# Attention state as four products of 144 columns over zeros, and the second route finished ahead of the third

## Chip, cores and metric

The kernel runs on one NeuronCore of a Trainium2 chip. The metric is device microseconds of one execution. Engines are named as in the profile: PE is TensorE (PEld its weight loads), DVE VectorE, ACT ScalarE, POOL GpSimd, SP SyncE.

## What is computed

Three layers follow one another: attention with a decay per head and no softmax (4 batches, 8 heads, 576 positions, 64 columns a head), a routed expert layer (2304 tokens of 512, 8 experts of width 1024, the best one only), and a gated FFN of width 1536.

```
scores = scale * np.matmul(q, k.transpose(0, 1, 3, 2))
Dmat = np.where(rel >= 0, gamma[:, None, None] ** rel[None, :, :], 0.0)
x = np.matmul(scores * Dmat, v)           # -> (2304, 512)
...
xn = x / (norm(x) + 1e-06)                # expert_idx = argmax(xn @ en.T / tau)
out[mask] = gate_w[mask, None] * (np.maximum(x[mask] @ w1[e], 0.0) @ w2[e])
...
return (silu(x @ w_gate) * (x @ w_val) @ w_out)
```

## The kernel before

**Attention.** A batch's 576 positions are cut into five chunks, four of 128 and one of 64 (c = 0 to 4), so that there are 20 chunks in all. The eight heads form four pairs (NP = 4): the pair's two heads of 64 columns lie on partitions 0 to 63 and 64 to 127 of q and k. The decay is put into two factors, `dk` on v's rows and `dq` on the output's rows. Beside the 64 columns of v each head carries 8 columns with its part of the expert logits (HE = 72), which `votes` makes.

For a chunk, `qk` (L231) makes the scores of all heads and VectorE multiplies them by the causal mask into `pd` (L244). `state` (L284) adds the chunk's k and v into a state in PSUM, and ScalarE copies it to SBUF as `sd` (L297), two buffers in turn. `rows` (L247) makes the output of the chunk: for c > 0 the queries times the state of the chunks before (L261), eight products, one for each head on its own 64 partitions, then the chunk's own scores times v (L265). VectorE then evicts the logits (L279), the rows (L281) and sums the logits over the heads (L282). PE instructions on float32 appear in the trace twice for each product written, each with a weight load.

**Order.** The schedule is written out by hand: `tc.manual_schedule()` keeps each engine's instructions in the order of the Python program. Step i of the main loop (L608) runs qk(i), votes, rows(i - 1), state(i), the preparation of v for chunk i + 2 on GpSimd (L215) and the load of chunk i + 5 on SyncE's queue, six chunk buffers in all.

**Routes.** A `Route` takes some chunks of a batch to their places in the experts' lists. `choose` (L316) finds the expert of each token on VectorE, after the root of the sum of squares on GpSimd (L325). `rank` counts the tokens ahead of each on PE. `place` turns that into row numbers, `weigh` makes the gate weight, and `scatter` (L392) sends the rows of a chunk out with one indirect DMA of GpSimd. The last batch is split into three routes: chunks 0 and 1, within the loop; 2 and 3 (`rb`); and 4 (`rc`). Where several generators are given to `run`, they are issued in turns, an instruction of each.

**After the attention.** `warm` issues bf16 products whose result is not used, 18 behind the last rank, 20 behind the branch that follows. SyncE then loads the first expert's rows, which waits for all scatters; the rows are scaled, transposed (L736) and split into two float32r parts. Eight experts and the FFN follow.

Of the kernel before, what the change touches and what calls it, by code (L numbers as in the profile page):

```python
# [4 lines left out]
F32 = mybir.dt.float32  # L5
# [47 lines left out]
def build(tc, main, tail, emb, wexp, keep, small, lim, wffn, out):  # L53
# [116 lines left out]
    sd = [ac.tile([P, NP, HE], F32, name=f"sd{i}") for i in range(2)]  # L170
# [60 lines left out]
    def qk(i):  # L231
        c = i % NC_
        L = CH[c][1]
        t = ck[i]
        t["pd"] = []
        scs = [ps_sc.tile([P, NP, P], F32, tag="sc", name="sc") for _ in range(2)]
        for p in range(NP):
            for a, sc in enumerate(scs):
                r = slice(64 * a, 64 * a + 64)
                nc.tensor.matmul(sc[keys(c, a), p, :L], t["k"][r, p], t["q"][r, p], start=True, stop=True)  # L240
        for a, sc in enumerate(scs):
            ks = keys(c, a)
            pd = ap.tile([P, NP, P], F32, tag=f"pd{a}", name="pd")
            nc.vector.tensor_tensor(out=pd[ks, :, :L], in0=sc[ks, :, :L], in1=causal[ks, P - L if a else 0:P if a else L].unsqueeze(1).to_broadcast([L, NP, L]), op=ALU.mult)  # L244
            t["pd"].append(pd)

    def rows(i, pool=None):  # L247

        b, c = divmod(i, NC_)
        L = CH[c][1]  # L250
        t = ck[i]
        if pool:
            parts = [pool.tile([P, 1, 512], F32, tag="sc", name="po") for a in range(2)]
# [12 lines left out]

        t = bt[b]
        lw = ap.tile([P, 2, NP, E], F32, tag="lw", name="lw")
        xv = t["xr"][:L, c, 0:D].rearrange("l (p a d) -> l a p d", p=NP, a=2)
        dqv = dq_s[:L, c].rearrange("l (p a) -> l a p", a=2)  # L270
        at = 0
        todo = []
        for x in parts:
            m = x.shape[1]
            s = slice(at, at + m)
            at += m
            view = x[:L, :, 0:NP * HE].rearrange("l a (p w) -> l a p w", p=NP)
            todo.append((xv[:, s], view[:, :, :, 0:HD], dqv[:, s].unsqueeze(3).to_broadcast([L, m, NP, HD])))
            nc.vector.tensor_tensor(out=lw[:L, s], in0=view[:, :, :, HD:HE], in1=dqv[:, s].unsqueeze(3).to_broadcast([L, m, NP, E]), op=ALU.mult)  # L279
        for o, x, y in todo:  # L280
            nc.vector.tensor_tensor(out=o, in0=x, in1=y, op=ALU.mult)  # L281
        nc.vector.tensor_reduce(out=t["lg"][:L, c], in_=lw[:L].rearrange("l a p e -> l e a p"), axis=AX.XY, op=ALU.add)  # L282

    def state(i):  # L284
# [12 lines left out]
        nc.scalar.activation(out=sd[(i + 1) % 2], in_=st, func=AF.Copy)  # L297
# [11 lines left out]
    class Route:  # L309


        def __init__(self, b, lo, hi):
            self.b, self.lo, self.n = b, lo, hi - lo
            self.L = max(CH[c][1] for c in range(lo, hi))

        def choose(self):  # L316
# [5 lines left out]
            mx, cm, dn, nrm = (ap.tile([P, NC_], F32, tag=x, name=x)[:L, :n] for x in ("mx", "cm", "dn", "nrm"))  # L322
# [15 lines left out]
            self.ex, self.dn, self.nrm = ex, dn, nrm  # L338
# [234 lines left out]
    with tc.manual_schedule():  # L573
# [10 lines left out]
        nc.gpsimd.memset(enb, 0.0)  # L584
        nc.scalar.activation(out=ej, in_=emb_s, func=AF.Square, accum_out=ess[:, 0:1])
# [22 lines left out]
        for i in range(N - 1):  # L608
# [59 lines left out]
        run(rc.weigh(), look_far(ac))  # L668
# [228 lines left out]
def _constants():  # L897
# [7 lines left out]
    dk = g[None, None, :] ** -at.astype(np.float64)  # L905
    dq = sc * g[None, None, :] ** at
# [55 lines left out]
```

## Times and profile before

| | us |
|---|---|
| runs of the kernel before | 819.76, 818.22, 823.55 (median 819.76) |
| the profiled execution's own time | 825.41 |
| its span, first to last instruction | 823.7 |
| granted clock of PE, mean of the span | 0.985 |

The profile is of one execution. Times in its rows count from the start of the span. [...] Busy times on PE overlap, as products are pipelined, so the spacing of starts says more than the sum.

### The profile page before, as it was taken

The numbers are of one execution on the slowest core, as the hardware profiler recorded it, in microseconds if no ns is written. First come the engines' busy times: TensorE is split into PE (matmuls) and PEld (weight loads), VectorE is DVE, ScalarE is ACT, GpSimd is POOL, SyncE is SP. The second block draws the span as 40 slices with busy tenths as digits, with TensorE's granted clock in tenths as the row PEclk, the third lists the DMA queues.
The fourth block names the chain that finished last, engine by engine and source line by source line (L and its number), as shares of the span: only waits on it lengthen the run. The fifth ranks groups of instructions, "written<-read, shape, count | busy, mean of one in ns | idle before, by whom it ended". The sixth has DMA issues, their size and how long they took to land.

```text
span 823.7 us, 14428 instructions
## 1 busy us (share of the span) xinstructions
PE 793.0 (96%) x5861; PEld 742.3 (90%) x5862; DVE 452.9 (55%) x866; ACT 258.8 (31%) x486; POOL 155.0 (19%) x154
## 2 busy tenths in 40 slices
PE   8897978999999999999999999999999999999995
PEld 5887838999999999999999999999999999999994
DVE  3565657566556566677744742772476356323322
ACT  2121226445444444444433311331232122111110
POOL 3354423111121011122201200120021011001122
PEclk9999989999999999999999999999999999999998
DMA  9999246554564454332211200120021000000121
GB/s 351 383 317 318 105 144 218 182 186 132 167 208 139 163 192 145 128 103 103 78 52 42 87 26 1 62 92 1 2 101 52 1 26 1 1 1 38 39 77 76
DMA packets 30312, 93.47 MB, mean 113 GB/s; under 512 B 5053, under 2 KB 5182, under 8 KB 30242
## 3 DMA queue, kind: packets, MB, share of 16 engines
q1 hardware_dynamic: 25552, 81.83, 29.2%
q0 software_dynamic: 4240, 9.85, 3.3%
q8 instruction: 47, 0.77, 0.3%
q10 hardware_dynamic: 450, 0.84, 0.3%
q14 instruction: 23, 0.19, 0.1%
HBM read 82.00 MB, written 11.97 MB: 114 GB/s over the span
## 4 chain that ended last, share of the span: by engine, by line
PE 71%; issue 17%; DMA 4%; DVE 3%; POOL 3%; ACT 0%; POOLq 0%; ACTq 0%; SPq 0%; DVEq 0%
PE po L862 13%; PE pg L750 9%; PE pg L751 9%; PE pg L749 9%; PE py L749 5%; PE py L750 4%; PE py L751 4%; PE ph L749 4%; PE ph L751 4%; PE ph L750 4%; DMA xs<-xr,slot 2%; PE po L265 2%; PE sc L240 2%; POOL out L870 2%; PE po L261 1%
## 5 line engine op out<-in xcount | busy, mean ns | idle before, releaser
L750 PE MATMUL pg<-yl,w 128*128 128x384 f32 x576 | 193.0, 335 | 0.0
L751 PE MATMUL pg<-yh,w 128*128 128x384 f32 x576 | 192.7, 335 | 0.0
L749 PE MATMUL pg<-yh,w 128*128 128x384 f32 x576 | 192.7, 335 | 0.0
L862 PE MATMUL po<-w,hh 128*128 128x512 f32 x432 | 135.7, 395 | 0.0
L852 DVE TENSOR_TENSOR hf<-pg,hf 128x384 f32<-128x384 f32 x72 | 40.2, 558 | 172.6 <-PE pg L751 168.4
L750 PEld LDWEIGHTS pg<-yl,w 128*128 128x128 f32 x576 | 108.1, 188 | 3.0
L749 PEld LDWEIGHTS pg<-yh,w 128*128 128x128 f32 x576 | 108.1, 188 | 2.9
L136 POOL TENSOR_TENSOR w<-w,w 128x512 fp32r<-128x512 f32 x36 | 50.8, 1410 | 310.7 <-DVE hl L854 235.7
L751 PEld LDWEIGHTS pg<-yh,w 128*128 128x128 f32 x576 | 108.1, 188 | 0.0
L114 DVE TENSOR_TENSOR w<-raw,w 128x1024 fp32r<-128x1024 f32 x64 | 78.3, 1224 | 36.3 <-ACT w L113 35.0
L862 PEld LDWEIGHTS po<-w,hh 128*128 128x128 f32 x432 | 80.3, 188 | 13.5 <-ACT hh L853 0.3
L851 ACT ACTIVATE hf<-pg 128x384 f32<-128x384 f32 x72 | 35.5, 493 | 169.2 <-PE pg L751 169.2
L853 ACT ACTIVATE hh<-hf 128x384 fp32r<-128x384 f32 x72 | 38.0, 527 | 159.2 <-DVE hf L852 159.2
L862 PE MATMUL po<-w,hl 128*128 128x512 f32 x216 | 85.6, 396 | 0.0
L749 PE MATMUL py<-hh,w 128*128 128x320 f32 x256 | 81.6, 319 | 0.0
L750 PE MATMUL py<-hl,w 128*128 128x320 f32 x256 | 79.8, 312 | 0.4 <-DVE hl L767 0.4
L751 PE MATMUL py<-hh,w 128*128 128x320 f32 x256 | 79.8, 312 | 0.0
L749 PE MATMUL ph<-xh,w 128*128 128x320 f32 x252 | 77.9, 309 | 0.0
L750 PE MATMUL ph<-xl,w 128*128 128x320 f32 x252 | 77.8, 309 | 0.0
L751 PE MATMUL ph<-xh,w 128*128 128x320 f32 x252 | 77.8, 309 | 0.0
L113 ACT ACTIVATE w<-raw 128x1024 fp32r<-128x1024 f32 x64 | 66.8, 1055 | 25.2 <-PE py L751 16.7
L854 DVE TENSOR_TENSOR hl<-hf,hh 128x384 fp32r<-128x384 f32 x72 | 40.2, 559 | 42.8 <-ACT hh L853 42.8
(133 smaller groups left out, 1118.7 us busy)
## 6 DMA issues: line engine op xcount, KB each, us to landing
raw<-wexp SPq DMA_DIRECT2D x64, 512.0 KB
raw<-wffn SPq DMA_DIRECT2D x36, 512.0 KB
ck<-main SPq DMA_DIRECT2D x32, 512.0 KB
xrow<-xs SPq DMA_DIRECT2D x16, 257.0 KB
ck<-main SPq DMA_DIRECT2D x16, 256.0 KB
ck<-tail SPq DMA_DIRECT2D x4, 512.0 KB
xrow<-xs SPq DMA_DIRECT2D x8, 128.5 KB
ck<-tail SPq DMA_DIRECT2D x4, 256.0 KB
```

What stands on the lines that cost most here:

```text
L113: nc.scalar.activation(out=w[:, 0], in_=raw, func=AF.Copy)
L114: nc.vector.tensor_tensor(out=w[:, 1], in0=raw, in1=w.bitcast(F32)[:, 0], op=ALU.subtract)
L136: nc.gpsimd.tensor_tensor(out=w[:, 1, i], in0=ff, in1=w.bitcast(F32)[:, 0, i], op=ALU.subtract)
L240: nc.tensor.matmul(sc[keys(c, a), p, :L], t["k"][r, p], t["q"][r, p], start=True, stop=True)
L749: nc.tensor.matmul(ps, w[0], ah, start=start, stop=False)
L750: nc.tensor.matmul(ps, w[0], al, start=False, stop=False)
L751: nc.tensor.matmul(ps, w[1], ah, start=False, stop=stop)
L851: nc.scalar.activation(out=hf, in_=pss[0], func=AF.Silu)
L852: nc.vector.tensor_tensor(out=hf, in0=pss[1], in1=hf, op=ALU.mult)
L853: nc.scalar.activation(out=hh, in_=hf, func=AF.Copy)
L854: nc.vector.tensor_tensor(out=hl, in0=hf, in1=hh.bitcast(F32), op=ALU.subtract)
L862: nc.tensor.matmul(po[t], h[a][:, s], w[:, c, f], start=(f == 0 and i == 0), stop=(f == 1 and i == 2))
```

## The change

The state in SBUF gets a place for both heads of a pair side by side, with zeros where a head's columns meet the other head's partitions. So one product of the pair's 128 partitions with 144 moving columns gives both heads, four products where there were eight. ScalarE copies the state in two halves; GpSimd zeroes both buffers at the start. The output's heads lie four to a PSUM bank in their order, instead of even heads in one and odd in the other. In the last chunk of a batch both heads' masked scores share one tile of 128 partitions, `dk` has zeros for the other head, and here too four products of 144 columns take the place of eight of 72.

The second change is in the routes of the last batch. The root is a step of its own (`root`), issued for the second route ahead of the first route's last scatter, which moves from step 18 to the steps behind the loop. The second route's choice stands ahead of the last chunk's rows; its place, weight and scatters come ahead of the third route's choice.

```diff
-    sd = [ac.tile([P, NP, HE], F32, name=f"sd{i}") for i in range(2)]
+    sd = [ac.tile([P, NP, 2, HE], F32, name=f"sd{i}") for i in range(2)]
...
+            if a == 0 or c < NC_ - 1:
+                pd = ap.tile([P, NP, P], F32, tag=f"pd{a}", name="pd")
...
-        bank = [x[:, a, 0:NP * HE].rearrange("l (p w) -> l p w", p=NP) for x in parts for a in range(x.shape[1])]
+        bank = [x[:, n, 0:4 * HE].rearrange("l (h w) -> l h w", w=HE) for x in parts for n in range(x.shape[1])]
         if c:
             for p in range(NP):
-                for a in range(2):
-                    r = slice(64 * a, 64 * a + 64)
-                    nc.tensor.matmul(bank[a][:L, p], t["q"][r, p, :L], sd[i % 2][r, p], start=(p == 0), stop=False, skip_group_check=True)
-        for p in range(NP):
-            for a in range(2):
-                for m in HALVES[:L // 64]:
-                    nc.tensor.matmul(bank[a][m, p], t["pd"][a][keys(c, a), p, m], t["vd"][keys(c, a), 2 * p + a], start=(c == 0 and p == 0), stop=(p == NP - 1), skip_group_check=True)
+                nc.tensor.matmul(bank[p // 2][:L, 2 * (p % 2):2 * (p % 2) + 2], t["q"][:, p, :L], sd[i % 2][:, p], start=(p % 2 == 0), stop=False, skip_group_check=True)
+        for p in range(NP):
+            o = bank[p // 2][:, 2 * (p % 2):2 * (p % 2) + 2]
+            if c < NC_ - 1:
                 for a in range(2):
+                    for m in HALVES:
+                        nc.tensor.matmul(o[m, a], t["pd"][a][:, p, m], t["vd"][:, 2 * p + a], start=(c == 0 and p % 2 == 0 and a == 0), stop=(p % 2 == 1), skip_group_check=True)
+            else:
+
+                nc.tensor.matmul(o[:L], t["pd"][0][:, p, :L], t["vd"][:, 2 * p:2 * p + 2], start=False, stop=(p % 2 == 1), skip_group_check=True)
...
-        nc.scalar.activation(out=sd[(i + 1) % 2], in_=st, func=AF.Copy)
+        for a in range(2):
+            r = slice(64 * a, 64 * a + 64)
+            nc.scalar.activation(out=sd[(i + 1) % 2][r, :, a], in_=st[r], func=AF.Copy)
...
+        def root(self):
+
+            if self.nrm is None:
+                n, L = self.n, self.L
+                self.nrm = ap.tile([P, NC_], F32, tag="nrm", name="nrm")[:L, :n]
+                nc.gpsimd.tensor_tensor(out=self.nrm, in0=bt[self.b]["ss"][:L, self.lo:self.lo + n], in1=half[:L, :n], op=ALU.pow)
...
-            nc.gpsimd.tensor_tensor(out=nrm, in0=t["ss"][:L, cs], in1=half[:L, :n], op=ALU.pow)
+            self.root()
...
+        for x in sd:
+            nc.gpsimd.memset(x, 0.0)
...
-                    at_step(i + 1 + (n if b < B - 2 else n // 2), lambda r=r, n=n: r.scatter(n))
+                    at_step(i + 1 + (n // 2 if b == B - 2 else n), lambda r=r, n=n: r.scatter(n))
 
         rb, rc = Route(B - 1, 2, 4), Route(B - 1, 4, 5)
         rows(N - 2)
         squares(N - 2)
+        rb.root()
         for fn in later.pop(N - 1, ()):
             fn()
+
+        run(rb.choose())
         rows(N - 1, ps_sc)
-        run(rb.choose())
         squares(N - 1)
         rb.rank()
-        run(rc.choose(), rb.place())
-        rc.rank(ps_sc)
-        run(rb.weigh(), rc.place(1))
+        rc.root()
+        run(rb.place(), rb.weigh())
         rb.scatter(0)
         rb.scatter(1)
-        run(rc.weigh(), look_far(ac))
+        run(rc.choose())
+        rc.rank(ps_sc)
+        run(rc.place(2), rc.weigh(), look_far(ac))
         rc.scatter(0)
         warm(WARM[1], ps_1.tile([P, 512], F32, tag="st", name="warm"))
...
+    half = (i[:, None] < P // 2) == (np.arange(H)[None, :] % 2 == 0)
+    dk[:, NC_ - 1] *= half
```

## Rows read from the trace of the kernel before

**Rows 1.** The page: busy us of the engines (part 1), instruction queue (part 3).
```profile
PE 793.0 (96%) x5861; PEld 742.3 (90%) x5862; DVE 452.9 (55%) x866; ACT 258.8 (31%) x486; POOL 155.0 (19%) x154
...
q8 instruction: 47, 0.77, 0.3%
```

**Rows 2.** Busy by stretch: length, busy (instructions) per engine, PEclk, DMA share, GB/s.
```profile
20.32:26.44 6.12, 5.51 (x121) 5.08 (x122) 2.42 (x6) 1.12 (x3) 3.37 (x5) 1.00 1.03 401
72.45:79.74 7.29, 5.60 (x126) 5.14 (x126) 3.49 (x9) 1.75 (x5) 2.96 (x6) 1.00 0.95 330
79.74:86.77 7.03, 6.54 (x126) 6.00 (x126) 4.28 (x15) 1.02 (x3) 2.23 (x2) 0.76 0.69 249
86.77:93.20 6.43, 5.81 (x125) 5.18 (x125) 3.12 (x18) 1.27 (x4) 2.45 (x3) 1.00 0.12 45
```

**Rows 3.** PE's waits, 14 to 90 us: waiter, waited for, total us, times, longest.
```profile
PE po L265 <- issue: 2.3, 3, 0.9
PE pu L224 <- issue: 2.2, 2, 1.7
PE po L261 <- issue: 1.7, 1, 1.7
PE pr L364 <- issue: 1.6, 1, 1.6
PE st L296 <- DVE vd L225: 1.1, 1, 1.1
PE sc L240 <- issue: 0.8, 2, 0.4
```

**Rows 4.** PE in order of time (start, length, what): rows of chunks 16, 19.
```profile
89.42 1.02 PE L261 MATMUL po<-sd,ck 64*128 64x72 f32 x16
90.36 1.22 PE L265 MATMUL po<-vd,pd 128*64 128x72 f32 x32
...
101.53 0.72 PE L261 MATMUL po<-sd,ck 64*64 64x72 f32 x16
102.08 0.67 PE L265 MATMUL po<-vd,pd 64*64 64x72 f32 x16
```

**Rows 5.** PE's transposes of the first rows: in time; the tile's list (ns min/median/max).
```profile
118.29 0.60 PE L736 MATMUL ptx<-keep_s,xrow 128*128 128x128 f32 x4
...
L736 PE MATMUL ptx<-keep_s,xrow x12: 222/272/328, 118.3 to 120.4; 128*128 128x128 f32 x8, 64*128 64x64 f32 x4
```

**Rows 6.** In order of time: ACT's state copy, POOL at the start; brackets: idle before.
```profile
4.78 0.57 POOL L586 TENSOR_TENSOR ess<-ess,half 8x1 f32<-8x1 f32 x1 [2.95 <-ACT ej L585]
21.98 0.53 POOL L633 MEMSET zrow<- 128x514 f32 x1
61.61 0.41 ACT L297 ACTIVATE sd<-st 128x288 f32<-128x288 f32 x1 [2.67 <-PE st L296]
```

**Rows 7.** In order of time: the end of attention, the warm products, the last transposes.
```profile
102.38 0.26 DVE L282 TENSOR_REDUCE lg<-lw 128x8 f32<-128x64 f32 x1
104.05 0.15 DVE L326 TENSOR_REDUCE mx<-lg 128x2 f32<-128x16 f32 x1
105.09 0.18 PE L364 MATMUL pr<-oh,tri_s 128*128 128x8 bf16 x1 [2.34 <-DVE cm L332]
106.49 6.93 PE L571 MATMUL warm<-ones 128*128 128x512 bf16 x18
107.69 0.15 DVE L354 RECIPROCAL xr<-sm 128x2 f32<-128x2 f32 x1
110.75 0.92 POOL L394 DMA_INDIRECT xs<-xr,slot  x1 [0.30 <-issue]
113.94 4.51 PE L571 MATMUL warm<-ones 128*128 128x512 bf16 x20 [0.52 <-PEq L478]
120.14 0.46 PE L736 MATMUL ptx<-keep_s,xrow 64*128 64x64 f32 x4 [0.62 <-DVE xrow L705]
```

**Rows 8.** Busy by stretch, columns as in rows 2: most of the 18 warm products.
```profile
105.56:112.37 6.81, 6.09 (x16) 2.21 (x16) 4.50 (x30) 2.43 (x4) 3.34 (x4) 0.50 0.31 106
```

More of the change, by code (lines that the diff above doesn't have):

```diff
@@ L242, in qk @@
             ks = keys(c, a)
-            pd = ap.tile([P, NP, P], F32, tag=f"pd{a}", name="pd")
+            if a == 0 or c < NC_ - 1:
+                pd = ap.tile([P, NP, P], F32, tag=f"pd{a}", name="pd")
             nc.vector.tensor_tensor(out=pd[ks, :, :L], in0=sc[ks, :, :L], in1=causal[ks, P - L if a else 0:P if a else L].unsqueeze(1).to_broadcast([L, NP, L]), op=ALU.mult)
-            t["pd"].append(pd)
+            if a == 0 or c < NC_ - 1:
+                t["pd"].append(pd)
     def rows(i, pool=None):
@@ L252, in rows @@
         if pool:
-            parts = [pool.tile([P, 1, 512], F32, tag="sc", name="po") for a in range(2)]
+            parts = [pool.tile([P, 1, 512], F32, tag="sc", name="po") for _ in range(2)]
         else:
             parts = [ps_1.tile([P, 2, 512], F32, tag="po", name="po")]
-        bank = [x[:, a, 0:NP * HE].rearrange("l (p w) -> l p w", p=NP) for x in parts for a in range(x.shape[1])]
+        bank = [x[:, n, 0:4 * HE].rearrange("l (h w) -> l h w", w=HE) for x in parts for n in range(x.shape[1])]
         if c:
             for p in range(NP):
+                nc.tensor.matmul(bank[p // 2][:L, 2 * (p % 2):2 * (p % 2) + 2], t["q"][:, p, :L], sd[i % 2][:, p], start=(p % 2 == 0), stop=False, skip_group_check=True)
+        for p in range(NP):
+            o = bank[p // 2][:, 2 * (p % 2):2 * (p % 2) + 2]
+            if c < NC_ - 1:
                 for a in range(2):
-                    r = slice(64 * a, 64 * a + 64)
-                    nc.tensor.matmul(bank[a][:L, p], t["q"][r, p, :L], sd[i % 2][r, p], start=(p == 0), stop=False, skip_group_check=True)
-        for p in range(NP):
-            for a in range(2):
-                for m in HALVES[:L // 64]:
-                    nc.tensor.matmul(bank[a][m, p], t["pd"][a][keys(c, a), p, m], t["vd"][keys(c, a), 2 * p + a], start=(c == 0 and p == 0), stop=(p == NP - 1), skip_group_check=True)
+                    for m in HALVES:
+                        nc.tensor.matmul(o[m, a], t["pd"][a][:, p, m], t["vd"][:, 2 * p + a], start=(c == 0 and p % 2 == 0 and a == 0), stop=(p % 2 == 1), skip_group_check=True)
+            else:
+                nc.tensor.matmul(o[:L], t["pd"][0][:, p, :L], t["vd"][:, 2 * p:2 * p + 2], start=False, stop=(p % 2 == 1), skip_group_check=True)
         t = bt[b]
-        lw = ap.tile([P, 2, NP, E], F32, tag="lw", name="lw")
-        xv = t["xr"][:L, c, 0:D].rearrange("l (p a d) -> l a p d", p=NP, a=2)
-        dqv = dq_s[:L, c].rearrange("l (p a) -> l a p", a=2)
+        lw = ap.tile([P, 2, 4, E], F32, tag="lw", name="lw")
+        xv = t["xr"][:L, c, 0:D].rearrange("l (n h d) -> l n h d", n=2, h=4)
+        dqv = dq_s[:L, c].rearrange("l (n h) -> l n h", n=2)
         at = 0
@@ L276, in rows @@
             at += m
-            view = x[:L, :, 0:NP * HE].rearrange("l a (p w) -> l a p w", p=NP)
-            todo.append((xv[:, s], view[:, :, :, 0:HD], dqv[:, s].unsqueeze(3).to_broadcast([L, m, NP, HD])))
-            nc.vector.tensor_tensor(out=lw[:L, s], in0=view[:, :, :, HD:HE], in1=dqv[:, s].unsqueeze(3).to_broadcast([L, m, NP, E]), op=ALU.mult)
+            view = x[:L, :, 0:4 * HE].rearrange("l n (h w) -> l n h w", h=4)
+            todo.append((xv[:, s], view[:, :, :, 0:HD], dqv[:, s].unsqueeze(3).to_broadcast([L, m, 4, HD])))
+            nc.vector.tensor_tensor(out=lw[:L, s], in0=view[:, :, :, HD:HE], in1=dqv[:, s].unsqueeze(3).to_broadcast([L, m, 4, E]), op=ALU.mult)
         for o, x, y in todo:
             nc.vector.tensor_tensor(out=o, in0=x, in1=y, op=ALU.mult)
-        nc.vector.tensor_reduce(out=t["lg"][:L, c], in_=lw[:L].rearrange("l a p e -> l e a p"), axis=AX.XY, op=ALU.add)
+        nc.vector.tensor_reduce(out=t["lg"][:L, c], in_=lw[:L].rearrange("l n h e -> l e n h"), axis=AX.XY, op=ALU.add)
     def state(i):
@@ L321, in choose @@
             r8b = r8_s[:L].unsqueeze(1).to_broadcast([L, n, E])
-            mx, cm, dn, nrm = (ap.tile([P, NC_], F32, tag=x, name=x)[:L, :n] for x in ("mx", "cm", "dn", "nrm"))
+            mx, cm, dn = (ap.tile([P, NC_], F32, tag=x, name=x)[:L, :n] for x in ("mx", "cm", "dn"))
             cd, ex = (ap.tile([P, NC_, E], F32, tag=x, name=x)[:L, :n] for x in ("cd", "ex"))
             oh = self.oh = ap.tile([P, NC_, E], BF16, tag="oh", name="oh")[:L, :n]
-            nc.gpsimd.tensor_tensor(out=nrm, in0=t["ss"][:L, cs], in1=half[:L, :n], op=ALU.pow)
+            self.root()
             nc.vector.tensor_reduce(out=mx, in_=lg, axis=AX.X, op=ALU.max)
@@ L337, in choose @@
             yield
[L338 removed]
+            self.ex, self.dn = ex, dn
         def weigh(self):
```

1 line of the change is left out of this document (added).

## Prediction

> **What bounds the kernel now.** I read the page first, then a table of busy time by stretch, then TensorE's own waits, then the instructions in order of time at two places. The page gives TensorE (PE) 96% of the span [rows 1]. That average holds two different stages: from about 120 us on the expert and FFN products follow each other closely and nothing of the change touches them; up to about 103 us the attention chunks run, and there the change acts. So I look at the first stage alone.
>
> In the table by stretch the reader should look at the counts, not at the busy time: between one standstill of PE and the next lie about 126 products and 126 weight loads, each time, whatever the products are [rows 2]. The table of PE's waits says what ends these standstills: of 9.7 us between 14 and 90 us, 8.6 stand under "issue" (the engine waited for nothing that the profile shows), 1.1 under VectorE, none under a transfer of q, k or v [rows 3]. The page has one more line that fits: the queue q8 brought 47 packets of instructions, 0.77 MB, while PE ran 5861 products and 5862 loads in all; that is 249 instructions for each packet [rows 1], and 252 lie between two standstills (semaphore instructions make up the small rest). I take it that PE runs out of instructions: in this stage a block of some 250 takes as long as the next one needs to arrive. Three of these blocks measure 6.12, 7.29 and 7.03 us; from 20.32 to 86.77 there are ten, 66.45 us, 6.64 each [rows 2]. Without the 9.7 us of waits PE would execute a block in 5.7 us. In the block after 86.77 the DMA share is 0.12 instead of 0.69 or more, and PE is busy for 5.81 of 6.43 us where it was 5.60 of 7.29 [rows 2]: from there I take it as bound by what it executes.
>
> [...]
>
> **The change, part by part.**
>
> *Products of the state (c = 1 to 3, twelve times).* Before, eight products of 72 columns, recorded as 16; 0.94 us from the first to the next line's first [rows 4]. After, four products of 144 columns over 128 rows, recorded as 8. A float32 product over the whole array is seen at the transposes: four of 128 columns take 0.60 us from the first start to the last end, and one alone 0.272, so their starts lie 0.109 apart and those of 144 columns would lie 0.122 apart [rows 5]; eight make 0.98. They no longer have the tile shape of the score products ahead of them. A change of shape costs between nothing and one product, 0.12; I take 0.1. Sum: +0.14 each.
>
> [...]
>
> *The last chunk of a batch (c = 4, four times).* Before, the state's 16 take 0.55 and those with the scores, by the same spacing, 0.50 [rows 4]. After, both kinds are eight of 0.122: 1.96. Sum: +0.9 each.
>
> *Instructions.* Each record has its weight load, so c = 1 to 3 drop 16 instructions and c = 4 drops 32. Up to 86.77 us the rows of nine chunks with c = 1 to 3 and three with c = 4 have run: 9 x 16 + 3 x 32 = 240 fewer, 0.95 of a block.
>
> *Sum from 20.32 to 86.77.* If arrival alone set the pace, 0.95 x 6.64 = 6.3 us would go. Execution grows, though: 66.45 - 9.7 = 56.8 us, plus 8 x 0.14 and 3 x 0.9 (one of the nine ran earlier), is 60.6 for 9.05 blocks, 6.7 each. Arrival and execution come out nearly equal, and each block takes the longer of the two; as the blocks with c = 4 execute longer than the others, I add 0.1: 9.05 x 6.8 = 61.5, a gain of 4.9. Bounds: 60.1 (all of arrival's share: -6.3) and every block at the last one's 7.03: 63.6 (-2.8).
>
> *From 86.77 to 101.5.* Three more chunks with c = 1 to 3, no arrivals to wait for: +0.4.
>
> *State's copy, zeros, one pd tile.* ScalarE's copy of the state was one of 0.41 us and becomes two on half the partitions; the work per partition is the same, so I take 0.41 each, +6.6 us in all, on an engine that waited 2.67 us ahead of this one [rows 6]; the state is read a chunk later. If that cover were gone it would cost 0.41 a chunk. The two memsets of 576 columns ahead of the embedding's root cost about 0.6 each by the memset of 514 columns (0.53); GpSimd idles 2.95 us there [rows 6], so nothing. Output in another order (heads four to a bank) leaves VectorE's element counts as they were: nothing; a worse stride would show in its eviction.
>
> *The end of attention.* Now VectorE evicts the rows of the last chunk (until 104.05) before the second route's selection; its rank starts at 105.09 [rows 7]. Afterwards selection starts when the logits of chunk 18 are there, 102.38 + 0.26 = 102.64, and the last chunk's rows come behind it; PE's longer c = 4 products (+0.9) are hidden under that 1.0 us. Selection and eviction together end about 105.1 as before, and from there the second route's steps go without the third's between them: weights at about 106.7 instead of 107.84 [rows 7], an estimate that gives the third route's steps 1.1 of the 2.75 us. The root of the second route moves on GpSimd ahead of the first route's last scatter; it waits for chunk 18's squares, and behind it queue that scatter and the third root; the scatters of the second route need the weights anyhow, so I cost this at nothing, and at one scatter's 0.92 + 0.30 us [rows 7] if the squares are late. Only then comes the third route: selection 1.0, rank 0.3, its place and weights. Its scatter issues at about 109.6, not 110.75: -1.1 for SyncE, which loads the rows of the first expert once all scatters have landed.
>
> But PE's 18 warm products stand behind the third rank, and this moves from 106.49 to about 106.7 + 1.3 = 108.0, +1.5. [...] Their end holds back the transposes; PE had 0.7 us to spare there (it waits 0.62 for the last tile, 120.14). 1.5 - 0.7 = +0.8 if the clock does what it did; -1.1 if it rises early; +1.6 if all 18 run at the low level (18 x 2 x 0.22). I take +0.6. Behind it the first expert's order on VectorE and its weight loads shift by the same.
>
> **Sum.** -4.9 + 0.4 + 0.6 = -3.9 us. The profiled execution took 825.41 us (span 823.7) and would become 821.5. It lies 5.65 above the median of the runs, 819.76; applied to that, 815.9.
>
> **The rivals.**
>
> *Waits shorter without the profiler.* I don't know where the 5.65 us lie. If all of it is in the arrivals, 8.6 shrink to 3.0, and before is nearly bound by execution: 56.8 + 1.1 + 3.0 = 60.9 against 60.6 + 0.5 after, so +0.2 + 0.4 + 0.6 = +1.2: 821.0. For it: the excess is of the size of these waits. Against it: no row says that it lies there.
>
> *Slower.* The waits may not go with the count of instructions: something else that recurs (a semaphore the profile doesn't show), or a boundary that costs the same however long the block was. Then nine waits stay and execution's growth is all that is left: 1.1 + 2.7 + 0.4 + 0.6 = +4.8, 824.6. It decides from the point where the stretches between waits no longer hold 252 instructions. Against it: the counts are alike in all stretches [rows 2]. [...]
>
> *The end pays as well.* Clock up early in the warm products: -4.9 + 0.4 - 1.1 = -5.6, 814.2.
>
> **How the numbers follow.** The first case 0.55, shorter waits 0.2, slower 0.12, the end pays 0.13. The first's own range is -6.3 + 0.4 - 1.2 to -2.8 + 0.4 + 1.6, 812.7 to 819.0; with the second case the range is 812.8 to 821.0, which leaves the slower rival and the lowest corner outside. About 1% (8.2 us) is what a measurement here can tell from no change; no case reaches it alone. Beyond -8.2 only the lowest corner with a spell of low clock gone, 0.05; beyond +8.2 the slower rival with a late second root, 0.02.
>
> **What would show it.** Right: the standstills of PE still lie 126 products apart, but there is one fewer by 82 us and most are below 0.5 us; the state's eight records take about 0.98; rows of chunk 18 start about 4.5 us earlier; the last scatter follows its third rank by 1.6, and the warm products start about 1.5 us later behind chunk 18's rows than before. Wrong: standstills as long and as many as before, state products far from 1 us, VectorE's or ScalarE's waits where PE's were, or the transposes of the first expert earlier behind the scatters than now.

## Result and the profile after

The kernel after takes 815.21 us (median of 10 runs, 813.62 to 817.19) where the kernel before, run beside it, takes 821.24 (10 runs, 818.22 to 824.36). The ratio is 0.9909, 95% interval 0.9889 to 0.9929: between 5.8 and 9.1 us less (the two medians alone lie 6.0 apart). The profiled execution took 815.26 us, span 813.6, against 825.41 and 823.7.

The page of the kernel after, busy time of the engines and the instruction queue, answers [rows 1]. There are 162 products and 160 loads fewer, one instruction packet fewer, and ScalarE is busy for 6.8 us more:

```profile
PE 790.8 (97%) x5699; PEld 741.6 (91%) x5702; DVE 453.2 (56%) x866; ACT 265.6 (33%) x502; POOL 158.1 (19%) x156
...
q8 instruction: 46, 0.75, 0.4%
```

The waits of PE from 14 to 90 us in the kernel after (waiter, waited for, us, times, longest) answer [rows 3]. This is the whole list; the 8.6 us under "issue" are gone, not shortened:

```profile
PE st L302 <- DVE vd L225: 1.1, 1, 1.1
```

Busy time by stretch in the kernel after, columns as in [rows 2], from one boundary of instruction blocks to the next (the count of PE's instructions gives where they lie). There are still 128 to 134 products to a block, but PE is busy all the time, and a block takes 5.07 us or 7.31, as its work goes; in the kernel before none of the ten from 20.32 to 86.77 took less than 6.00:

```profile
57.26:64.57 7.31, 7.31 (x128) 6.64 (x126) 5.33 (x22) 2.96 (x9) 4.83 (x6) 1.00 0.93 327
64.57:69.64 5.07, 5.07 (x130) 4.78 (x130) 2.08 (x8) 1.53 (x4) 2.85 (x3) 1.00 1.03 403
69.64:76.61 6.97, 6.96 (x134) 6.51 (x131) 5.64 (x18) 2.25 (x6) 3.13 (x6) 1.00 1.03 413
```

PE in order of time in the kernel after (start, length, what): the rows of chunk 17, then those of chunk 19, as in [rows 4]. The state's four products run from 79.47 to 80.64, 1.17 us (predicted 1.08); in the last chunk the two kinds start 0.98 apart, as predicted:

```profile
79.47 1.25 PE L262 MATMUL po<-sd,ck 128*128 128x144 f32 x8
80.64 1.22 PE L268 MATMUL po<-vd,pd 128*64 128x72 f32 x32
...
90.11 1.14 PE L262 MATMUL po<-sd,ck 128*64 128x144 f32 x8
91.09 1.14 PE L271 MATMUL po<-vd,pd 128*64 128x144 f32 x8
```

Where the 10.1 us between the two spans lie: the rows of chunk 18 (L265, L268) start at 89.06 instead of 100.38 us, 11.3 earlier; from there to the first expert product it takes 20.2 us instead of 20.6, another 0.4; but from that product to the first transpose of the second expert 23.2 instead of 21.2, 2.0 given back; the rest is alike within 0.4.

**What the prediction had passed over.** One of [rows 2] shows a mean clock of 0.76 in the kernel *before*, and I had not costed it. Busy time by stretch of the kernel before, columns as in [rows 2], and one of its PE lines from 40.7 to 43.9 us (busy us, mean ns):

```profile
40.70:43.90 3.20, 3.20 (x38) 3.07 (x36) 2.10 (x11) 0.85 (x3) 1.79 (x2) 0.50 0.59 227
81.70:85.00 3.30, 3.30 (x40) 2.93 (x38) 2.00 (x10) 1.02 (x3) 1.47 (x2) 0.50 0.86 338
```

```profile
L261 PE MATMUL po<-sd,ck 64*128 64x72 f32 x16 | 1.8, 406 | 0.0
```

Both stretches stand at a granted clock of 0.50, half of the full one. The first spell begins 1.3 us behind the end of a wait of 1.6 us, the second 1.9 us behind one of 1.7 (L364 and L261 in [rows 3]; the waits end at the boundaries at 39.3 and 79.74). In the first a product of the state takes 406 ns, where the mean from 20 to 87 us is 290. The kernel after has no such spell between 13 and 94 us. So two of this profile's late blocks were followed by slow products as well as by the wait (behind the first 406 ns against 290).

### The profile page after: what moved, and what is told of

Its sections match the earlier page's. It is cut to its first block, busy times and chain, and to the rows that moved or that the text cites. A ratio compares the mean times of both kernels' runs of the same rounds, so it can differ in the third digit from the quotient of the medians.

```text
span 813.6 us, 14126 instructions
## 1 busy us (share of the span) xinstructions
PE 790.8 (97%) x5699; PEld 741.6 (91%) x5702; DVE 453.2 (56%) x866; ACT 265.6 (33%) x502; POOL 158.1 (19%) x156
## 4 chain that ended last, share of the span: by engine, by line
PE 66%; issue 14%; DVE 2%; POOL 2%; DMA 1%; ACT 0%; POOLq 0%; DVEq 0%; ACTq 0%
PE po L883 13%; PE pg L771 9%; PE pg L772 9%; PE pg L770 9%; PE py L770 5%; PE py L771 4%; PE py L772 4%; PE ph L770 4%; PE ph L772 4%; PE ph L771 4%; POOL out L891 2%; DMA raw<-wexp 1%; PE ptx L745 1%; DVE w L114 1%; PE warm L587 1%
```

## Experiments

All views below take the same stretch: from the score products of chunk 3 to those of chunk 19, 16 steps of the loop. For each kernel stands the line of busy time by stretch, and for most the longest waits of PE within it. I compare with an undisturbed pace, the shortest of each step in the four profiles with the old products (before, e2, e5, e8; a wait of about 1 us left out of the one step in which none is free of it): 61.3 us for the 16 steps, an estimate that no single profile reaches. A batch's five steps take 3.23, 3.36, 4.09, 4.06 and 4.09; in the kernel after 3.36, 4.16 (the last chunk's), 4.08, 4.39 and 4.39, and it goes through all 16 without a wait, 66.42 us. The change thus executes 5.1 us *longer* here. Kernel before and kernel after, this stretch:

```profile
21.19:98.30 77.11, 67.54 (x1471) 62.40 (x1469) 45.25 (x159) 15.87 (x46) 37.62 (x45) 0.96 0.82 295
```

```profile
20.73:87.15 66.42, 66.41 (x1344) 61.70 (x1341) 45.92 (x159) 21.73 (x59) 36.87 (x45) 1.00 0.90 340
```

The experiments came in this order: e1 to e4 take the change apart and test the count of instructions; they left open whether the waits of the profiled execution were usual and what makes a block late, which e5 to e8 ask; e9 and e10 try a cure for it; e11 and e12 are the two predictions that followed from all this.

### e1, e2: the two halves of the change alone

e1 is the kernel before with the products, zeros, banks and tiles of the change, e2 the kernel before with its routes (the diff above, cut in two).

> The state's and the last chunk's products as in the change, the routes' order as before. If the arrival of PE's instructions is what the change relieves, nearly the whole gain is here: 5 to 6.5 us faster than before, and no wait on issue of more than 0.5 us between 14 and 90 us in the profile. If the order of the routes gave the gain: within 1.5 us of before. If execution set the pace, 3 to 4 us slower than before, since the products run longer.

> The routes' order as in the change, the products as before. If the gain is that of the products: within 1 us of before (the warm products start about 1.3 us later behind the last rows, the last scatter 1.5 earlier), and 8 to 9 us of waits on issue in the profile as before. If the order of the routes gave the gain: 5 to 6 us faster than before.

e1: 816.59 us, ratio 0.9936 (0.9914 to 0.9959). e2: 820.58, ratio 0.997 (0.9935 to 1.0004). The sum of the two, -0.94%, is what the whole change gives, -0.91%; by itself e2 is not told from no change, as its interval reaches 1. The stretch of e1, that of e2, and e2's waits:

```profile
19.44:85.77 66.33, 66.33 (x1343) 61.71 (x1340) 45.95 (x159) 21.76 (x59) 37.88 (x45) 1.00 0.91 348
```

```profile
21.64:92.81 71.17, 66.01 (x1471) 61.48 (x1468) 45.55 (x159) 15.59 (x46) 35.68 (x44) 0.95 0.85 311
```

```profile
PE pu L224 <- issue: 3.0, 2, 2.0
PE sc L240 <- issue: 1.1, 2, 0.6
PE po L265 <- issue: 1.0, 2, 0.7
```

The products alone take all waits away. In e2 the code up to chunk 16 is that of before: it is one more sample of it, with 5.1 us of waits and a spell of low clock from 68.6 us on.

### e3, e4: fewer instructions, or as many, by other means

e3 makes the votes with whole weights; e4 is the kernel after with each product of 144 columns written as two of 72.

```
 e3 (votes, before)
-            for m in HALVES:
-                nc.tensor.matmul(pu[m, p], t["vt"][:, p, m], enb[:, p], start=True, stop=True)
+            nc.tensor.matmul(pu[:, p], t["vt"][:, p], enb[:, p], start=True, stop=True)
 e4 (rows, after): bank[..][:L, 2 * (p % 2):2 * (p % 2) + 2] and sd[i % 2][:, p]
                   become two products, one for each a, on [:L, 2 * (p % 2) + a] and sd[i % 2][:, p, a]
```

> The kernel before, with one edit that the change does not have: the products that make the votes take a weight tile of 128 columns at once in place of two of 64, so 8 records a chunk in place of 16, 320 PE instructions fewer in all, while 128 columns of weights are loaded either way, so the execution stays within 0.1 us a chunk. If the count of instructions sets the pace: 4 to 6 us faster than before, though no product of the state has changed. If it is the state's products or the tile shape that matter: within 1.5 us of before.

> The changed kernel, each product of 144 columns written as two of 72 over the same 128 rows and the same weights: the same columns in all, so the execution is the same to 0.3 us a chunk, but 320 PE instructions more, as many as before the change. If the count of instructions sets the pace: the gain is gone, 5 to 9 us slower than the changed kernel (820 to 824), with waits on issue back in the profile. If the shape of the products or the full tile gave the gain: within 2 us of the changed kernel (815 to 817).

e3: 821.82 us, ratio 0.999 (0.9968 to 1.0011); the 4 to 6 us that I expected are missing. e4: 824.44, ratio 1.0035 (1.0014 to 1.0055), 9 us above the kernel after, more than the return of the waits. In both, execution grew by more than I had put down. The stretch of e3, and its votes (busy us, mean ns), then the state products of e4:

```profile
23.14:95.24 72.10, 72.03 (x1336) 67.19 (x1333) 47.11 (x160) 15.59 (x46) 35.48 (x43) 1.00 0.85 303
```

```profile
L223 PE MATMUL pu<-enb,ck 128*128 128x16 f32 x128 | 17.2, 265 | 0.1
```

```profile
L263 PE MATMUL po<-sd,ck 128*128 128x72 f32 x128 | 16.0, 278 | 0.0
L263 PE MATMUL po<-sd,ck 128*64 128x72 f32 x48 | 3.6, 229 | 0.0
```

In e3 a product of 16 columns takes 17.2/128 = 0.134 us of PE where it took 9.7/240 = 0.040 with a weight half as wide: eight of these start 0.995 apart from the next line where sixteen took 0.437, +0.56 per chunk. There is no wait left, and the stretch takes 72.1, all of it executed. In e4 a product of 72 columns with a 128-column weight takes 16.0/128 = 0.125, hardly less than one of 144 (12.5/80 = 0.156 in the kernel after): the state's part of a full chunk goes from 1.18 to 1.94 us, and twelve times 0.76 is 9.1, about all of the loss. Its profile, of the slowest of ten runs, has one wait of 1.4 us under issue besides and a spell of low clock (mean clock of the stretch 0.96). So e4 did not test the count, it priced the wide weight. e3 tells more: in this stretch alone it executes 10.8 us longer than the undisturbed 61.3, and yet its time is that of before. About as much of the kernel before must be time in which PE executes nothing, or slowly.

### e5: the kernel before, once more

> The kernel before, profiled once more. Theory (each block of some 252 PE instructions has to arrive in time): waits under issue in 14 to 90 us again, at the same counts of products, 5 to 9 us in all, and the span follows their sum: with 5 us of waits about 820, with 8.6 about 823.7. Rival (the profiled execution of before was odd, and a usual one has few such waits): under 3 us of issue waits.

One run, 822.27 us, span 820.6. Its stretch, its waits, and its time at low clock:

```profile
21.15:95.00 73.85, 67.60 (x1471) 63.28 (x1468) 45.67 (x159) 15.58 (x46) 36.62 (x45) 0.93 0.84 305
...
40.80:50.60 9.80, 9.80 (x121) 9.51 (x120) 3.85 (x19) 1.87 (x6) 5.32 (x5) 0.50 0.88 286
```

```profile
PE pr L364 <- issue: 2.4, 1, 2.4
PE pu L224 <- issue: 2.2, 2, 1.3
```

Waits of 6.2 us in the stretch where the first profile had 9.6, and ten microseconds at a granted clock of 0.50 behind the longest of them, 2.4 us, where it had 6.8 in two spells. What is lost differs from execution to execution, but it is always there: 77.1, 73.9 and 71.2 us (e2) against 61.3 undisturbed. The first profiled execution was the worst of the three; the rival by which a usual one has less than 3 us of waits is out.

### e6: more instructions that do next to nothing

Kernel before, 16 products of one column ahead of each chunk's votes:

```
+        for n in range(16):
+            m = HALVES[n % 2]
+            nc.tensor.matmul(pu[m, 0, 0:1], ones[:, m], ones[:, 0:1], start=True, stop=True)
```

> The kernel before with 16 more products per chunk ahead of the votes, each of one moving column and a 64-column bf16 weight, written into a place that the votes overwrite: 32 instructions per chunk, 640 in all, 2.5 blocks of 252. Such products start 0.025 us apart in the ranks of before, so execution grows by 0.4 per chunk, 8.0 in all. Theory (a block takes the longer of its execution and the arrival of the next one): before is bound by arrival, so the count sets the time: 2.5 blocks at 6.25 to 6.64 us are +15 to +17, and waits under issue stay or grow; +10 if the arrival gets shorter with less work between. Rival 1 (the waits recur for another reason and take up what execution grows by): 0 to +2. Rival 2 (the waits stay as they are beside the execution): +8.

833.23 us, ratio 1.0105 (1.0044 to 1.0165), between 3.6 and 13.6 us more.

```profile
21.47:107.14 85.67, 75.02 (x1744) 70.39 (x1741) 45.66 (x160) 15.58 (x46) 37.34 (x45) 0.90 0.77 266
```

```profile
PE st L299 <- issue: 4.5, 2, 3.0
PE pr L366 <- issue: 2.5, 1, 2.5
```

The waits stay (10.7 us in all) and do not take up the added execution: rival 1 is out. That execution is 0.28 per chunk by the rows (0.25 from the first added product to the votes, and votes 0.03 longer), not the 0.4 that I had put. In the profile the time goes with the count: 6.2 us for 252 instructions (85.67 x 252 / 3485), and 6.6, 6.3 and 6.1 in the three profiles of the old products; but it is the profile of the slowest of four runs, and part of its time is low clock (mean 0.90). By the runs the theory's first figure, +15 to +17, is out; its +10 for a shorter arrival and rival 2's +8 (5.6 with 0.28 per chunk) both lie within the interval, and between these e6 doesn't decide.

### e7: the last chunk's pairs back

Kernel after, but for c = 4 the body of `rows` is that of before, banks and eviction too, with these two products:

```
+        if c == NC_ - 1:
+            return rows_last(i, pool)
...
+                    nc.tensor.matmul(bank[a][:L, p], t["q"][r, p, :L], sd[i % 2][r, p, a], start=(p == 0), stop=False, skip_group_check=True)
...
+                    nc.tensor.matmul(bank[a][m, p], t["pd"][0][keys(c, a), p, m], t["vd"][keys(c, a), 2 * p + a], start=(c == 0 and p == 0), stop=(p == NP - 1), skip_group_check=True)
```

> The kernel after, but the last chunk of each batch goes back to pairs of half arrays, heads apart by bank as before; chunks 1 to 3 keep the 144-column products. In the trace of after the two kinds of c = 4 take 1.03 and 0.74 to 0.98 us against 0.55 and 0.50 to 0.60 of before: 0.8 to 0.9 less execution per batch, 3.4 in all, against 32 more instructions each, 128 in all, half a block. Theory A (after is bound by execution, its waits are gone): -3.2 to -3.6 against after, about 811.7. Theory B (after stands at the floor of arrival, about 6.25 us per block): waits under issue come back, 1 to 3 us of them, and the time is that of after within 1.5 us.

815.05 us, ratio 0.9885 (0.9837 to 0.9933), the time of the kernel after within what can be told.

```profile
22.20:88.40 66.20, 64.80 (x1391) 59.58 (x1389) 46.02 (x159) 21.73 (x59) 35.40 (x43) 1.00 0.90 334
```

```profile
PE sc L240 <- issue: 1.4, 2, 0.8
```

Theory B. The three last chunks in the stretch execute 0.80 less each, 2.4 us, and 2.2 come back, 1.4 of them in listed waits. The kernel after stands just where execution and arrival meet.

### e8: the same instructions, less data

```
-                for a in (slice(0, 2), slice(2, 4), slice(4, 5)):
+                if i <= 6:
+                    nc.sync.dma_start(out=qk0 if i == 6 else t[:, 0:2], in_=src[:, 0:2])
+                for a in (slice(2, 4), slice(4, 5)):
                     nc.sync.dma_start(out=t[:, a], in_=src[:, a])
+            if i >= 6:
+                ck[i] = dict(q=heads(qk0[:, 0]), k=heads(qk0[:, 1]), vt=heads(t[:, 2]), v=t[:, 3], kt=t[:, 4])
+                return
```

> The kernel before with less to load: from chunk 6 on, all full chunks use the q and k of chunk 6, so that 0.52 of each 1.31 MB is not loaded (q and k of the later full chunks are left out of the computation); PE's instructions, their order and shapes are those of before. Theory (instruction packets start 3.6 to 4.9 us after a boundary because they queue behind the data of the chunks): the packets start 1 to 2.5 us after it, waits under issue from 40 us on fall below 1 us, -5 to -8. Rival (arrival takes its time whatever is loaded): waits as in before, within 1.5 us of it.

813.64 us, ratio 0.9883 (0.9822 to 0.9945): 9.6 us less than before (4.5 to 14.7), with every PE instruction of before.

```profile
20.86:86.31 65.45, 62.86 (x1472) 58.66 (x1469) 45.45 (x159) 15.57 (x46) 36.26 (x44) 1.00 0.77 262
```

```profile
PE po L271 <- issue: 0.8, 2, 0.4
PE pu L230 <- issue: 0.7, 1, 0.7
PE sc L246 <- issue: 0.6, 2, 0.4
PE pr L370 <- issue: 0.5, 1, 0.5
```

This is the decisive run. Counts, order and shapes are those of before (1472 products), the DMA share is 0.77 instead of 0.82 to 0.85 and the rate 262 GB/s instead of 295 to 311; the waits fall to 2.6 us, none above 0.9, and no spell of low clock follows. By the records of queue q8, a packet starts 1.0 to 3.6 us after a boundary here and 3.7 to 4.9 in the kernel before (1.2 there too at 86.77, when the loads have ended and the DMA share is 0.12); it takes 0.95, and PE goes on 1.2 to 1.5 us behind its end. I had expected starts 1 to 2.5 us after a boundary. An example of before, the DMA queues (packets, MB, share of 16 engines) behind the boundary at 72.45, first from 72.5 to 77.3 us, then from 77.3 to 78.4; PE waits until 79.74:

```profile
q1 hardware_dynamic: 423, 1.24, 75.6%
q0 software_dynamic: 106, 0.34, 17.4%
...
q8 instruction: 1, 0.02, 5.2%
```

One more reading of these waits was open: that PE waits for q or k, of which e8 loads less, and the profile doesn't say so. But in e8, and in the kernel before up to 86.77 us, each wait under issue of the stretch comes when the count of PE's products and loads has grown by 252 or a multiple of it since the last, in the middle of one line's products as well as between lines. One of them in the chain of the kernel before, in order of time, start and length:

```profile
25.62 0.43 PE sc L240 x9
26.05 0.39 issue
26.44 0.45 PE sc L240 x7
```

### e9, e10: one chunk buffer less

Kernel before (e9), and before with the routes (e10):

```
-    cq = tc.alloc_tile_pool(name="chunks", bufs=6)
+    cq = tc.alloc_tile_pool(name="chunks", bufs=5)
...
-                for a in (slice(0, 2), slice(2, 4), slice(4, 5)):
+                for a in (slice(2, 4), slice(0, 2), slice(4, 5)) if i > 3 else (slice(0, 2), slice(2, 4), slice(4, 5)):
...
-            if i + 5 < N:
-                load_chunk(i + 5)
+            if i + 4 < N:
+                load_chunk(i + 4)
```

> The kernel before with five chunk buffers in place of six, the load of a chunk one step later (i + 4 instead of i + 5), v ahead of q and k: as many bytes, but one chunk less (1.3 MB, about 3.2 us at 410 GB/s) standing in the queues at any time. PE's instructions are those of before. Theory 1 (an instruction packet waits behind the data that are already queued): packets start 1 to 3 us after a boundary instead of 3.6 to 4.9, waits under issue in 14 to 90 us fall from 8.6 to under 4, -4 to -7. Theory 2 (what delays the packet is the share of time in which the DMA engines are busy, and the bytes to move are the same): waits as before, within 2 us of it. Rival (chunks come too late with one buffer less): waits for ck or vd, slower.

> Before with the change's routes alone (as e2, 820.6) and five chunk buffers. The undisturbed step of a full chunk takes 4.06 to 4.09 us with the old products and 4.39 with the new ones (last chunk's step 3.36 and 4.16), 61.3 against 66.2 us from the score products of chunk 3 to those of chunk 19. Theory 1 of the run above: waits mostly gone, the old products' shorter execution pays, 811 to 816, at or below the kernel after: then the change's products would have been worth nothing without the late instructions. Theory 2: as e2 within 2 us, above 818.

e9: 822.01 us, ratio 0.9983 (0.9957 to 1.0009). e10: 820.42, ratio 0.9957 (0.9937 to 0.9977), as e2. No cure.

```profile
19.46:94.00 74.54, 70.36 (x1471) 66.17 (x1469) 45.79 (x159) 15.58 (x46) 38.87 (x46) 0.89 0.86 314
```

In the median time theory 2 holds: less data standing in the queues is worth nothing when as much has to be moved. Inside, e9 is less clear. Packets start 0.7 to 4.3 us after a boundary, the waits come to 4.2 us instead of 5.1 to 9.6; but two of them (1.6 and 1.3 us) are followed by long spells at low clock, and the mean clock of the stretch is 0.89, the lowest of all. e10 keeps 5.3 us of waits, the longest 2.1, and one spell. What the queues' depth does to a packet is left open.

### e11: the change with less data

The kernel after with the loads of e8.

> The kernel after with the lighter loads of e8 (q and k of chunk 6 serve all later full chunks; those of the later chunks are left out of the computation). Theory (the change pays because blocks of instructions come late under the data's load, and after is bound by what it executes): nothing to gain here, within 2 us of the kernel after, so 0 to 3 us above e8 (813.6), whose old products execute 4.9 us less from the score products of chunk 3 to those of chunk 19 and keep 4.1 us of waits. The gain of the change, 6 to 8 us with full loads, is then gone. Rival (the change pays by itself, by the products, the evictions or the routes): 6 to 8 us below e8, about 806.

815.54 us, ratio 0.9898 (0.9861 to 0.9934); e8, with the old products, took 813.64. With full loads the change gains 6 to 8 us, with lighter ones nothing, and the kernel after does not care whether the data are loaded (815.21 and 815.54). Its stretch, with two waits of 0.4 us under issue:

```profile
19.26:87.12 67.86, 66.95 (x1343) 62.05 (x1340) 45.53 (x159) 21.77 (x59) 38.81 (x46) 1.00 0.76 268
```

What the change gains, it gains by late instructions that it avoids.

### e12: the weights' split ahead of time

What the kernel after gives back in the first expert had a reason that could be mended: PE's wait there, from the list of waits, 100 to 140 us, and then ScalarE, VectorE and PE in order of time, all of the kernel after:

```profile
PE ptx L745 <- DVE tv L732: 4.8, 1, 4.8
```

```profile
128.15 1.06 ACT L113 ACTIVATE w<-raw 128x1024 fp32r<-128x1024 f32 x1 [2.63 <-DMA raw<-wexp]
...
129.24 1.23 DVE L114 TENSOR_TENSOR w<-raw,w 128x1024 fp32r<-128x1024 f32 x1 [2.38 <-ACT w L113]
...
132.45 1.11 PE L745 MATMUL ptx<-keep_s,xrow 128*128 128x128 f32 x4 [4.79 <-DVE tv L732]
```

The weights' splits wait for loads, VectorE stands in order behind them, and the rows of the second expert come late. Three buffers hold the raw weights; until the attention is over nobody empties them.

```
             if i >= N - 6:
-                feed(0)
+                feed(int(i in (N - 4, N - 3)))
```

> The kernel after, but the first two weight tiles of the first expert are split into their two parts during chunks 16 and 17 instead of behind the attention; that frees their buffers, and two more tiles are loaded in the stretch from 80 to 102 us, in which the DMA engines stand nearly idle. In the kernel after the transposes of the second expert wait 4.8 us behind VectorE, whose splits wait for ScalarE's and these for loads issued from 103.9 us on. Theory (the first expert is bound by its weights' arrival): two tiles of 1.5 us each earlier, that wait falls from 4.8 to about 2, -2 to -3 against after. Rival 1 (the loads are not what is late): within 0.7 us of after. Rival 2 (the loads hold up the last blocks of instructions, or the splits VectorE's evictions): +1 to +2, with waits under issue or under VectorE between 78 and 92 us.

812.26 us, ratio 0.986 (0.9829 to 0.989): 3 us below the kernel after by the medians, the fastest kernel here whose loads are whole. The two were not run side by side; against the kernel before run beside each, the intervals (from 0.9829 to 0.989 and from 0.9889 to 0.9929) just touch, so the direction is likely and the size not settled. PE's transposes in e12, the first expert's and the second's:

```profile
112.28 1.03 PE L757 MATMUL ptx<-keep_s,xrow 128*128 128x128 f32 x8
...
132.59 0.60 PE L745 MATMUL ptx<-keep_s,xrow 128*128 128x128 f32 x4
```

From the first expert's transposes to the second's are 20.3 us where the kernel after needs 25.0 (107.42 to 132.45), and the wait of 4.8 is gone from the list. It isn't free: in this profile the attention ends 4.9 us later than in that of the kernel after, with waits of 0.7 and 0.4 us under issue and 0.5 under VectorE between 76 and 92 us, where the kernel after has none, and a spell of low clock (0.50) from 92.2 to 95.5. That is what rival 2 foresaw, beside the theory's gain. In this profile, of one of the two slowest of six runs, the two nearly cancel: 4.7 us won, 4.9 lost, the span 812.9 against 813.6. That the loss is smaller in a usual run is read from the median alone.

### All runs in one table

Execution per block is the undisturbed time of the stretch, divided by its blocks of 252 instructions (products and loads in the rows above). For e1, e3 and after it is the measured time, for e7 66.4 less three times 0.8, for e4 66.4 and ten times 0.76, for e6 61.3 and 16 times 0.28, for e11 and e12 that of after. Where a row stands for several kernels, their values follow in the order of their names.

| kernel | instructions | execution per block, us | waits under issue, us | mean clock | DMA, GB/s |
|---|---|---|---|---|---|
| e6 before, count up | 3485 | 4.8 | 10.7 | 0.90 | 266 |
| before, e5, e2 | 2940 | 5.3 | 9.6, 6.2, 5.1 | 0.96, 0.93, 0.95 | 295, 305, 311 |
| e9, e10, one buffer less | 2940, 2941 | 5.3 | 4.2, 5.3 | 0.89, 0.95 | 314, 315 |
| e8 before, less data | 2941 | 5.3 | 2.6 | 1.00 | 262 |
| e7 last pairs back | 2780 | 5.8 | 1.4 | 1.00 | 334 |
| after, e1 | 2685, 2683 | 6.2 | none, none | 1.00, 1.00 | 340, 348 |
| e12, e11 (less data) | 2683 | 6.2 | 0.8, 0.8 | 1.00, 1.00 | 337, 268 |
| e4 after, split | 2941 | 6.3 | 1.4 | 0.96 | 294 |
| e3 votes whole | 2669 | 6.8 | none | 1.00 | 303 |

With full loads the waits fall as a block's execution grows, and all but end at about 6 us; a packet that comes very late still shows behind a longer block, as in e4, where one started 4.8 us after its boundary and a wait of 1.4 us followed. A rate of bytes alone does not explain the waits (after and e1 move the most); a block that takes longer than its successor needs to come does. Why packets start sooner in the kernel after, at the higher rate, is not shown.

## Why the prediction was right, and where not

**The bound.** Right: PE ran out of instructions between 20 and 87 us. No record says so in words; it is read from the count of 252 between the waits and from the packets, behind whose ends PE goes on. (The small rest in the prediction's count is in the trace: 126 products, 126 loads and 4 semaphore instructions of PE from 26.44 to 32.69 us.) e8 and e11 show it from the side of the data (2.6 and 0.8 us of waits are left), e3 and e7 from that of the execution (none and 1.4). From a boundary to its packet are 3.7 to 4.9 us in this stretch; with 0.95 and 1.2 to 1.5 more that is 5.9 to 7.4, and a block of 5.3 us of work doesn't cover it. With the 1.2 us of the boundary at 86.77 the same sum gives 3.4 to 3.7, an estimate, and such a block would.

**State products.** +0.14 each predicted; the steps of a batch grow by 0.13, 0.33 and 0.30 with the full chunks and by 0.80 with the last, for which 0.9 was predicted. The spacing worked out from the transposes, 0.122, was too small: eight records take 1.17, 0.147 each. The 0.1 for the change of shape, for which the prediction gives no row, was right: the 16 score records of chunk 17 take 1.10 us to the start of the next line's products in the kernel after, whose shape is another, and 0.995 in the kernel before, whose shape is theirs (there too it is 1.09 where another shape follows, at 76.69 us). Over the stretch 5.1 us where my terms give 4.1 (ten times 0.14, three times 0.9).

**Sum from 20.32 to 86.77.** This is the term that was mis-sized: -4.9, bounds -6.3 and -2.8. The two kernels' rows of chunk 18 lie 11.3 us apart in the profiles; against e5 (96.87) it is 7.8, against e2 (94.69) 5.6. The term let each block take the longer of arrival and execution at one fixed arrival of 6.64 us. Two things were not in it. Behind some late blocks the clock was low: 6.8 us at 0.50 in the profile of before, ten in e5, none in the kernel after. Of the 15.8 us that the profile of before lies above the undisturbed 61.3, 9.6 are listed waits, the spells account for at most 3.4 (an estimate: half of the time at the lower level), and what the other 2.8 are no row says. And the arrival isn't fixed: in the kernel after blocks of 5.07 us come without a wait, as the packets start 1.1 to 4.4 us behind a boundary there; a packet's delay is not a constant (1.2 to 4.9 us in the kernel before, 1.0 to 3.6 with the lighter loads of e8).

**State's copy, zeros, banks.** Nothing, as predicted: ScalarE has 6.8 us more to do (predicted 6.6), no wait on it appears in the list; VectorE's time is 453.2 against 452.9.

**The end.** The steps came out as worked out. Counted from the first of chunk 18's state products (87.90 us in the kernel after, 99.33 before), the last scatter issues 1.5 us earlier than before (predicted 1.1), the warm products start 1.4 later (predicted 1.5), the first transposes 0.55 later (predicted 0.6). The end of attention in the kernel after, in order of time, answers [rows 7]; then SyncE's waits from 96 to 104 us:

```profile
96.49 6.13 PE L587 MATMUL warm<-ones 128*128 128x512 bf16 x17 [0.33 <-issue]
97.86 0.92 POOL L410 DMA_INDIRECT xs<-xr,slot  x1 [0.30 <-issue]
102.36 1.41 SPq L707 DMA_DIRECT2D xrow<-xs  x3
103.07 4.51 PE L587 MATMUL warm<-ones 128*128 128x512 bf16 x19 [0.45 <-PEq L494]
107.37 0.48 DVE L726 TENSOR_SCALAR xrow<-xrow 64x512 f32<-64x512 f32 x1 [1.72 <-DMA xrow<-xs]
107.42 1.42 PE L757 MATMUL ptx<-keep_s,xrow 128*128 128x128 f32 x12
```

```profile
SPq L494 <- SPq L494: 3.2, 1, 3.2
```

Only the end of the transposes was read wrongly: PE's last ones wait for the third tile of rows, and that comes with SyncE. It loads the rows 4.5 us after the last scatter's issue (3.6 before), since it stands 3.2 us behind the branch on L494 with nothing else shown; in the kernel before it stood 2.3 us behind that branch (L478), and then 1.2 us more for the last scatter's landing. So of the scatter's 1.5 us 0.6 are left, and the first expert product comes 0.3 earlier behind chunk 18's rows, not later. What SyncE waits for in the 3.2 us is not shown: five packets of another instruction queue, q14, come between 98.9 and 102.3 us, but no row says for which engine, and ScalarE goes on 0.4 us behind the same branch.

**Not in the sum at all.** The first expert: with the attention ended earlier its weights are no earlier, since their buffers are emptied only behind the branch. Of the gain 2.0 us go there in the profile; e12 takes 4.7 us out of this place, and pays for it ahead of it.

**The rivals.** *Waits shorter without the profiler* is out by e5 and e2 (6.2 and 5.1 us, with spells of low clock beside them); the 5.65 us by which the profiled execution lay above the median were partly in these waits, and even so most remain. *Slower* didn't come: the growth of execution that it counts up to 86.77 us (1.1 + 2.7) is there, measured 5.1 over the stretch, but no wait stayed. *The end pays as well* fell short: most of the 18 warm products ran at low clock again (0.51 from 94.2 to 101.1 us, as in [rows 8]). The prediction's terms for them rest on two levels, and the runs show both: in the two profiles they start 0.427 us apart at 0.50 and 0.218 at 1.00. No run shows all 18 at the low level, for which the prediction puts +1.6; in the kernel after the 17 recorded ones took 6.13 us. (18 x 2 x 0.22 is 7.9 us, 1.0 above the 6.93, and with the 0.8 it should have been +1.8, the upper bound 819.2. Nothing hung on it.)

**The number.** 815.9 predicted, 815.21 measured; but the difference was predicted as -3.9 and came out as -5.8 to -9.1. That the time fits so well is partly luck: the forecast was made against a median of three runs, 819.76, that lay 1.5 below the later one, and this made up for part of a gain that was put too small. The measured gain of 0.9% lies at the edge of what I called no change.

## What to carry to other kernels

Count an engine's instructions as a resource of its own where its pace is hundreds of short ones in a few microseconds (here 252 products and loads in 5.3 us): compare a block's execution with the time in which the next one comes under the load of that stretch, and make the products larger only until the two meet. Here that was at about 6 us a block: at 5.8 (e7) 1.4 us of waits were left, at 6.8 (e3) none, but the stretch took 72.1 us where the kernel after needs 66.4. Test such a theory from the side that the edit doesn't touch: taking data away with the instructions unchanged (e8), and the edit with the data away (e11), told more than any variation of the products. When a stage gets shorter, look for what was loaded or prepared in its shadow, here the first weights, and start that earlier.

## What the hardware showed

- From 16 us to the rows of the last chunk, eleven spells at a granted clock of 0.50 began at waits of PE under issue of 1.3 to 3.0 us, from 0.4 us ahead of the wait's end to 2.3 behind it (before, e2, e4, e5, e6, e9, e10); e12 has one more, behind shorter waits of 0.5 to 0.7. Five waits of 1.2 to 1.8 us had none behind them. In the profiles without a wait above 1.1 us there (after, e1, e3, e7, e8, e11) none began.
- With a weight of 128 columns a float32 product of 16 moving columns is no cheaper than one of 72: start to start 0.124 us for 16 columns (e3), 0.121 for 72 (e4), and 0.147 for 144 (after). With a weight of 64 columns, two side by side, 0.027 for 16 columns and 0.033 for 72. Undisturbed, the old pairs on half the rows took 0.94 us where the new products take 1.17, a factor of 1.25.
- An instruction packet (16,384 bytes in the records of q8) took 0.88 to 1.27 us itself between 14 and 90 us of the two kernels' profiles. What varied more is when it started: in the kernel before 1.2 us after the boundary at 86.77, in a stretch with a DMA share of 0.12, and 4.9 us after that at 72.45, with 0.95 and 330 GB/s.
